# A fused attention and FFN kernel: the first batch's k norms by a transposing sum, its first weight load in narrower pieces, its folds in other banks

## The chip, the cores and the metric

The kernel runs on one core of one Trainium2 chip. The metric is the device time of one execution in microseconds (us); the figure to go by is the median of several runs. Engines: PE is TensorE's matmul, PEld its weight loads, DVE is VectorE, ACT is ScalarE, POOL is GpSimd, SP is SyncE. Both POOL and SP issue DMA transfers here.

## What is computed

Four batches of cross-covariance attention, and then a feed-forward network with a product of two projections:

```python
def _attn_ref(q, k, v, tau):          # q, k, v: (4, 5824, 256)
    qn = q / (np.linalg.norm(q, axis=1, keepdims=True) + 1e-06)
    kn = k / (np.linalg.norm(k, axis=1, keepdims=True) + 1e-06)
    s = kn.transpose(0, 2, 1) @ qn / tau
    s = s - s.max(-1, keepdims=True)
    a = np.exp(s)
    a /= a.sum(-1, keepdims=True) + 1e-09
    return (v @ a).astype(np.float32)

def _moe_ref(x, w1, w2, w3, w_out):   # w1, w2: (256, 1024); w3: (1024, 1024); w_out: (1024, 256)
    a = x @ w1
    b = x @ w2
    h = a * b @ w3
    return (h @ w_out).astype(np.float32)
```

The norms run over the 5824 tokens, so each batch has 256 norms of q and 256 of k, and its attention matrix is only 256x256. tau is 1.

## The kernel before

Three products are folded ahead of time. The attention matrix e (exponentials, not yet divided by their sums) goes into the first weights: Wf = e w1 and e w2, with the division in the eviction from PSUM. And w3 w_out is one matrix, W_sb. What is left for a batch is a loop over chunks of 512 tokens and over eight blocks of 128 hidden columns: two products a and b of v's transposed tokens with Wf (`emit_ab`, L656), their elementwise product on DVE (abh, L673, after ACT has copied a, L662), and the product of abh with W_sb. One pass over one block is called a slot. While a batch's loop runs, the next batch's scores and norms are put between its slots.

**The first batch** has no loop to hide in. Its q and k come in six pieces by DMAs that POOL issues, with a cast from fp32 to bf16; TensorE forms the products G = q^T k (`products`, L271) and the squares of q (`squares`, L259, the 128x128 products of each half with itself, of which the diagonal is wanted) as they arrive. The squares of k take two ways. For pieces 0 to 3 and half of piece 4, ACT squares and DVE adds into `kacc` (`add_k_squares`); the rest goes to TensorE into S["k"] like q's.

Then follow the steps of `soft_units(0)`, taken in the order written out by hand at L853 to L873: soft0[7] is `k_early` (the two halves of kacc added to the row kk), soft0[0] `k_first` (the diagonal of S["k"] times the identity, plus kk), soft0[1] `k_row`, soft0[2] `q_first` (the diagonal of S["q"], dq), soft0[3] `scaled_first` (G times kr, the norms of q, both halves of the exponentials e), soft0[6] `sum_start`, and soft0[4] `first_folds`. `k_row` multiplies by a matrix of ones, so that each partition has all 256 sums of squares, and takes the reciprocal norms by Ln and Exp in four steps of ACT over 128x256, kr. The remaining steps of the first batch are set among the first slots of the loop by `make_agenda` (L907 and following): soft0[5], `second_quarter`, ahead of the second slot, and the four folds of columns 512 to 1023 after it.

`first_folds` makes the folds of columns 0 to 127 and 128 to 255 (`narrow_fold`), `second_quarter` those of 256 to 511, and `fold(i)` for i = 4 to 7 those of the last 512 columns: i = 4 and 5 for w1, 6 and 7 for w2. All of the narrow folds of columns 0 to 255 stand in TensorE's queue ahead of the first slot of the loop.

**Later batches** have their norms another way: `norms` (L301) is a VectorE sum that transposes 32x32 blocks and sums along them, `totals` multiplies the 16 columns with `fold4` (four stacked identities of 32), four ACT steps work on 16 columns, and `spread` (L322) transposes the norms of k back into a row.

**Loads.** POOL issues all loads in one queue, and each waits, by one of eight semaphores in turn, until the load eight before it has landed. w1 and w2 come in three pairs (L844 to L846): columns 0 to 255, 256 to 511 and 512 to 1023. Ahead of them is the first half of v's first piece, behind them the second half, v's pieces 1 and 2, w_out and w3. SP issues DMA transposes (w3, and v from piece 2 on) and the stores. In the loop, `at(t, ...)` sets a step at a time t of a clock that counts TensorE's planned work; `gate` and `hold` let POOL wait for the loop or for a transpose before it issues a load.

**PSUM banks** come from `bank(tag)`: four in turn for "ab" (a and b of the slots, and other short-lived tiles), three in turn for "out". A tile waits until its bank's last tile has been evicted. In the first batch, `fold(i)` has the default tag "ab".

Of the kernel before, what the change touches and what calls it, by code (L numbers as in the profile page):

```python
# [9 lines left out]
AF = mybir.ActivationFunctionType  # L10
ALU = mybir.AluOpType
F32 = DT.float32
BF16 = DT.bfloat16

P = 128
# [10 lines left out]
def kernel(  # L26
# [12 lines left out]
    nc = tc.nc  # L39

    B, N, C = q.shape
    T, D = out.shape
    F = moe_w1.shape[1]
# [24 lines left out]
    work = ctx.enter_context(tc.tile_pool(name="work", bufs=2))  # L68
# [6 lines left out]
    def bank(tag):  # L75

        turns[tag] += 1
        return {"tag": f"{tag}{turns[tag] % (4 if tag == 'ab' else 3)}", "bufs": 1}
# [7 lines left out]
    ones_pp = consts.tile([P, P], F32)  # L86
# [3 lines left out]
    eps_t = consts.tile([P, 1], F32)  # L90
# [6 lines left out]
    fold4 = consts.tile([P, 4, 32], F32)  # L97
# [21 lines left out]
    def load_part(nm, n, pi, lo, hi):  # L119
        nc.gpsimd.dma_start(  # L120
            out=pieces[nm, n, pi][:, lo:hi, :], in_=qk_main[nm, n][0][:, pi * PIECE + lo : pi * PIECE + hi, :]
        )
# [10 lines left out]
    def new_vT(n):  # L133
        vTs[n] = (
            vT_pool.tile([P, NT - 1, CT, P], BF16, tag="vT", name=f"vT_{n}"),
            vT_pool.tile([P, CT, P + LEFT], BF16, tag="vTt", name=f"vTt_{n}"),
        )
# [22 lines left out]
    def transpose_piece(n, pi):  # L160
        if pi == 0:
            new_vT(n)
        vT, vTt = vTs[n]
        t = pieces.pop(("v", n, pi))
        if pi < NP_ - 1:
            nc.sync.dma_start_transpose(vT[:, pi * PIECE : (pi + 1) * PIECE, :, :], t[:, :, :])
        else:
            g = LAST - 1
            nc.sync.dma_start_transpose(vT[:, pi * PIECE : pi * PIECE + g, :, :], t[:, :g, :])

            first = n % 2 == 0
            nc.sync.dma_start_transpose(vTt[:, :, :P] if first else vTt[:, :, LEFT:], t[:, g, :])
            nc.sync.dma_start_transpose(vTt[:, :, P:] if first else vTt[:, :, :LEFT], t[:LEFT, g + 1, :])
# [3 lines left out]
    accs = {}  # L177
# [57 lines left out]
    kacc = []  # L235
# [41 lines left out]
    def soft_units(n):  # L277
        st = {}

        def k_early():  # L280
            st["kk"] = work.tile([P, C], F32, tag="kk", name="kk", bufs=1)
            nc.vector.tensor_copy(st["kk"], kacc[0][:, 0, :])
            nc.vector.tensor_add(st["kk"], kacc[0][:, 1, :], st["kk"])

        def k_first():
            d = work.tile([P, CT, P], F32, tag="sq", name="dk", bufs=2)
            nc.vector.tensor_mul(d, S["k"], ident.unsqueeze(1).to_broadcast([P, CT, P]))
            d = st["ksq"] = d.rearrange("p c t -> p (c t)")
            nc.vector.tensor_add(d, d, st["kk"])

        def scaled_first():
            for ct in range(CT):
# [2 lines left out]
            exps(0)  # L295
            exps(1)

        def norms():

            red = work.tile([P, 16], F32, tag="red", name=f"red_{n}", bufs=1)  # L300
            nc.vector.tensor_reduce(  # L301
                out=red, in_=accs[n].rearrange("p w (b j) -> p (w b) j", j=32),
                axis=mybir.AxisListType.X, op=ALU.add, apply_transpose=True,
            )
            st["red"] = red

        def totals():
# [3 lines left out]
            )  # L311

        def norm_step(i):
            t = st["tot"][:, :16]
            nc.scalar.activation(
                out=t, in_=t, func=(AF.Ln, AF.Exp)[i % 2],
                scale=(1.0, 0.5, 1.0, -1.0)[i], bias=eps_t if i == 2 else 0.0,
            )

        def spread():  # L320
            st["kr"] = work.tile([P, C], F32, tag="kr", name=f"kr_{n}", bufs=1)
            nc.vector.transpose(  # L322
                st["kr"].rearrange("p (b j) -> p b j", j=32),
                st["tot"][:, 8:16].unsqueeze(2).to_broadcast([P, 8, 32]),
            )

        def pick():
# [9 lines left out]
        def k_row():  # L337

            m = psum.tile([P, 512], F32, name=f"row_{n}", **bank("ab"))
            nc.tensor.matmul(m[:, :C], lhsT=ones_pp, rhs=st["ksq"], start=True, stop=True)  # L340
            st["row"] = m[:, :C]
            st["kr"] = work.tile([P, C], F32, tag="kr", name=f"kr_{n}", bufs=1)
            for i in range(4):
                k_step(i)

        def k_step(i):
            kr = st["kr"]
            nc.scalar.activation(
                out=kr, in_=kr if i else st["row"], func=(AF.Ln, AF.Exp)[i % 2],
                scale=(1.0, 0.5, 1.0, -1.0)[i], bias=eps_t if i == 2 else 0.0,  # L350
            )

        def diagonal(src):
            d = work.tile([P, CT, P], F32, tag="sq", name=f"dq_{n}", bufs=2)
# [26 lines left out]
        def exps(ct):  # L381
            if ct == 0:
                st["e"] = work.tile([P, CT, C], BF16, tag="e", name=f"e_{n}", bufs=2)
            nc.scalar.activation(
                out=st["e"][:, ct, :], in_=st["s"][:, ct, :], func=AF.Exp, scale=st["r"][:, ct : ct + 1]
            )
# [51 lines left out]
        def fold(i, tag="ab"):  # L438
            h, rest = divmod(i, 4)
            w, c1 = divmod(rest, 2)  # L440
            for c2 in range(CT):
                fold_mm((w, c1, h * 512, (h + 1) * 512), c2, tag, i % 2 == 0 or (n == 0 and i == 7))
# [31 lines left out]
                    narrow_fold(256, 512, c1, c2)  # L474

        if n == 0:
            return [k_first, k_row, q_first, scaled_first, first_folds, second_quarter, sum_start, k_early] + [lambda i=i: fold(i) for i in range(4, 8)]

        return (
            [(0.0, 0.0, norms), (0.1, 2.4, totals)]  # L480
# [21 lines left out]
    def at(t, cost, fn):  # L502
        seq[0] += 1
        agenda.append((t, seq[0], cost, fn))
# [336 lines left out]
    load_piece("q", 0, 5, (1, 3, 4))  # L841
    new_piece("v", 0, 0)
    load_part("v", 0, 0, 0, half)
    for f0, f1 in ((0, 256), (256, 512), (512, F)):  # L844
        nc.gpsimd.dma_start(out=w12[:, :, 0, f0:f1], in_=w1r[:, :, f0:f1])
        nc.gpsimd.dma_start(out=w12[:, :, 1, f0:f1], in_=w2r[:, :, f0:f1])  # L846
    load_part("v", 0, 0, half, PIECE)
# [59 lines left out]
    def make_agenda(b):  # L907
        agenda.clear()
        clock[0] = 0.0
        n = b + 1  # L910
        if b == 0:
            at(0.5, 0.87, soft0[5])
            for i in range(4):
                at((1.7, 2.6, 3.5, 3.9)[i], 0.43, soft0[8 + i])
            at(4.6, 0.5, lambda: transpose_half_on_pe(0, 0, 1, False))
            at(7.0, 0.5, lambda: transpose_half_on_pe(0, 1, 0, False))
            at(8.0, 0.5, lambda: transpose_half_on_pe(0, 1, 1, False))
            at(15.0, 0.0, transpose_w3)
            at(15.0, 0.0, lambda: transpose_piece(0, 2))
            for jt in range(FT):  # L920
                at(28.3 + 1.2 * jt, 0.87, lambda jt=jt: w_unit(jt))
            moves = [("qk", 1, 0, 29.0), ("qk", 1, 1, 29.2), ("v", 0, 3, 33), ("qk", 1, 2, 49), ("qk", 1, 3, 56)]
            moves += [("qk", 1, 4, 62), ("v", 0, 4, 68), ("qk", 1, 5, 79), ("v", 0, 5, 88)]
            moves += [("v", 1, 0, 99), ("v", 1, 1, 110), ("qk", 2, 0, 122)]
        else:
            moves = [("qk", n, 1, 1), ("v", b, 2, 7), ("qk", n, 2, 19), ("v", b, 3, 25), ("qk", n, 3, 37)]
            moves += [("v", b, 4, 43.5), ("qk", n, 4, 55.5), ("v", b, 5, 61), ("qk", n, 5, 72.5)]
            moves += [("v", n, 0, 85), ("v", n, 1, 98), ("qk", n + 1, 0, 111)]
            moves = [m for m in moves if m[1] < B]

        for nm, m, pi, t in moves:
            if nm == "qk" and m == 1 and pi in (0, 2):
                at(t, 0.0, lambda pi=pi: hold(vTs[0][0][:1, (2 + pi // 2) * PIECE, 0, :1]))
            at(t, 0.0, gate)
            if nm == "qk":
                at(t, 0.0, lambda m=m, pi=pi: load_qk(m, pi))
            else:
                at(t, 0.0, lambda m=m, pi=pi: load_piece("v", m, pi))
                at(t + 4.0, 0.0, lambda m=m, pi=pi: transpose_piece(m, pi))
        if b == 0:  # L940
            for i in range(4):
                at(COMB + 2.6 * i, 0.0, lambda i=i: combine_weights(i))
        if n == B:
            agenda.sort()
            return
        units = score_units(n)
        soft = soft_units(n)
        first, last = SLOTS if b > 0 else SLOTS0
        for s in range(first, last):
            lo_, hi_ = (share(b, x, first, last, len(units)) for x in (s, s + 1))  # L950
            by_slot.append((s, units[lo_:hi_]))

        def chain():
            for cst, t, fn in soft:
                at(clock[0] + 1.0 + t, cst, fn)
            agenda.sort()

        by_slot.append((last, [(0.0, chain)]))
        agenda.sort()
# [23 lines left out]
    n = len(pend)  # L983
# [37 lines left out]
```

## Time and profile before

| | us |
|---|---|
| median of 3 runs | 556.74 (555.41 to 557.5) |
| the profiled execution | 555.64 |
| its span, first to last instruction | 553.9 |
| first product of the loop (L656) starts | 37.12 |
| PE busy in the span | 542.9 (98%) |
| DVE, ACT, POOL busy | 435.3, 377.0, 305.5 |

The share of busy time is over the whole span. The page's row of DMA engines by fortieths shows how different the start is:

```profile
PE   8799999999999999999999999999999999999997
DMA  9999889986666878676554777865650245443102
```

Each digit is a slice of 13.8 us, in tenths. In the first four slices the DMA engines are at nine tenths or more; later they have room. A landing is the moment when a transfer's last packet is in; "issue" in the chain of waits is time in which nothing that the profile shows was waited for.

### The profile page before, as it was taken

The numbers are of one execution on the slowest core, as the hardware profiler recorded it, in microseconds if no ns is written. First come the engines' busy times: TensorE is split into PE (matmuls) and PEld (weight loads), VectorE is DVE, ScalarE is ACT, GpSimd is POOL, SyncE is SP. The second block draws the span as 40 slices with busy tenths as digits, with TensorE's granted clock in tenths as the row PEclk, the third lists the DMA queues.
The fourth block names the chain that finished last, engine by engine and source line by source line (L and its number), as shares of the span: only waits on it lengthen the run. The fifth ranks groups of instructions, "written<-read, shape, count | busy, mean of one in ns | idle before, by whom it ended". The sixth has DMA issues, their size and how long they took to land.

```text
span 553.9 us, 12324 instructions
## 1 busy us (share of the span) xinstructions
PE 542.9 (98%) x4623; PEld 353.3 (64%) x4630; DVE 435.3 (79%) x787; ACT 377.0 (68%) x757; POOL 305.5 (55%) x259
## 2 busy tenths in 40 slices
PE   8799999999999999999999999999999999999997
PEld 4564577766666666666667666666666666666665
DVE  5558747899976787988876788888877688888984
ACT  5446647788866777777766777777766666566663
POOL 4260021877889678889887588898987400010000
PEclk9999999999999999999999999999999999999999
DMA  9999889986666878676554777865650245443102
GB/s 214 211 178 209 168 160 207 214 206 90 160 130 155 191 150 162 126 148 138 127 128 121 153 152 158 167 141 120 151 115 40 83 114 119 92 111 80 77 40 96
DMA packets 75260, 77.61 MB, mean 140 GB/s; under 512 B 54208, under 2 KB 59072, under 8 KB 75200
## 3 DMA queue, kind: packets, MB, share of 16 engines
q0 software_dynamic: 15904, 38.93, 40.0%
q1 hardware_dynamic: 58928, 37.17, 24.5%
q8 instruction: 36, 0.59, 0.4%
q10 hardware_dynamic: 368, 0.72, 0.4%
q14 instruction: 24, 0.20, 0.1%
HBM read 78.91 MB, written 23.86 MB: 186 GB/s over the span
## 4 chain that ended last, share of the span: by engine, by line
PE 92%; DMA 6%; POOL 1%; DVE 0%; ACT 0%; issue 0%; POOLq 0%
PE a L656 28%; PE b L656 28%; PE prodA L569 12%; PE prodC L569 6%; PE G L200 5%; PE prodB L569 3%; DMA k<-in_k_dram 3%; PE o L704 3%; PE fold L427 2%; DMA q<-in_q_dram 2%; PE o_out L735 2%; PE w L878 1%; DMA w<-in_moe_w_dram 1%; PE narrow L451 0%; DVE abh L673 0%
## 5 line engine op out<-in xcount | busy, mean ns | idle before, releaser
L673 DVE TENSOR_TENSOR abh<-as,b 128x512 bf16<-128x512 bf16 x352 | 240.2, 684 | 82.9 <-ACT as L662 77.8
L662 ACT CAST as<-a 128x512 bf16<-128x512 f32 (+1 forms) x384 | 215.4, 562 | 93.7 <-PE a L656 61.5
L656 PE MATMUL a<-vT,Wf 128*128 128x512 bf16 x704 | 209.6, 380 | 0.1
L656 PE MATMUL b<-vT,Wf 128*128 128x512 bf16 x704 | 209.7, 380 | 0.0
L656 PEld LDWEIGHTS <-Wf 128*128 128x128 bf16 x1536 | 141.0, 98 | 100.7 <-issue 0.5
L569 PEld LDWEIGHTS <-S 128*128 128x128 bf16 x1248 | 82.6, 98 | 34.3
L212 DVE TENSOR_TENSOR acc<-acc,sq 128x512 f32<-128x512 f32 x132 | 91.6, 694 | 3.0 <-ACT sq L197 1.9
L579 ACT COPY osb<-prodA 128x256 f32<-128x256 f32 x156 | 58.1, 372 | 42.0 <-PE prodA L569 41.4
L588 POOL TENSOR_TENSOR S<-abh,abh 128x1024 bf16<-128x1024 bf16 x29 | 61.7, 2127 | 31.5 <-DVE abh L673 16.6
L569 PEld LDWEIGHTS <-abh 128*128 128x128 bf16 x936 | 61.9, 98 | 25.7 <-issue 0.2
L591 POOL TENSOR_TENSOR S<-S,abh 128x1024 bf16<-128x1024 bf16 x29 | 61.7, 2126 | 1.9
L591 POOL TENSOR_TENSOR S<-abh,S 128x1024 bf16<-128x1024 bf16 x29 | 61.8, 2133 | 0.1
L591 POOL TENSOR_TENSOR S<-abh 128x1024 bf16<-128x1024 bf16 x29 | 61.8, 2131 | 0.1
L644 POOL COPY gate_t<-abh 1x1 bf16<-1x1 bf16 x39 | 7.2, 185 | 79.9 <-DVE abh L673 79.7
L569 PE MATMUL prodA<-comb_T,S 128*128 128x128 bf16 x624 | 47.6, 220 | 0.0
L200 PE MATMUL G<-k,q 128*128 128x256 bf16 x276 | 47.0, 273 | 0.0
L197 ACT ACTIVATE sq<-q 128x512 f32<-128x512 bf16 x69 | 43.8, 634 | 0.0
L197 ACT ACTIVATE sq<-k 128x512 f32<-128x512 bf16 x69 | 43.4, 628 | 0.0
L582 DVE TENSOR_TENSOR osb<-prodC,osb 128x256 f32<-128x256 f32 x78 | 32.5, 417 | 0.0
L648 POOL COPY gate_t<-vT 1x1 bf16<-1x1 bf16 x2 | 0.4, 176 | 53.3 <-DMA vT<-v 53.3
L200 PEld LDWEIGHTS <-q 128*128 128x128 bf16 x276 | 23.9, 98 | 3.6
L569 PE MATMUL prodB<-W_sb,abh 128*128 128x128 bf16 x312 | 23.8, 220 | 0.1
(137 smaller groups left out, 469.8 us busy)
## 6 DMA issues: line engine op xcount, KB each, us to landing
out_dram<-osb SPq DMA_DIRECT2D x44, 512.0 KB, 3.3
k<-in_k_dram POOLq DMA_DIRECT2D x19, 512.0 KB, 8.7
v<-in_v_dram POOLq DMA_DIRECT2D x19, 512.0 KB, 5.6
q<-in_q_dram POOLq DMA_DIRECT2D x18, 512.0 KB, 5.4
w_wout<-in_moe_w_dram POOLq DMA_DIRECT2D x1, 2048.0 KB, 22.4
k<-in_k_dram POOLq DMA_DIRECT2D x4, 320.0 KB, 7.0
v<-in_v_dram POOLq DMA_DIRECT2D x4, 320.0 KB, 5.2
q<-in_q_dram POOLq DMA_DIRECT2D x3, 320.0 KB, 5.0
```

Source lines behind the costliest of these rows:

```text
L197: nc.scalar.activation(out=sqs[0][:, :, part, :], in_=src[:, o : o + 2, :], func=AF.Square)
L200: nc.tensor.matmul(G[:, ct, :], lhsT=qt[:, i, ct * P : (ct + 1) * P], rhs=kt[:, i, :], start=(pr == 0 and part == 0 and ct == 0), stop=(pr ...
L212: nc.vector.tensor_add(accs[n], accs[n], sqs[0][:, part - 2])
L569: nc.tensor.matmul(st[nm][:, i, :], lhsT=a[:, j, i * P : (i + 1) * P], rhs=w[j], start=(first and j == 0 and i == 0), stop=(j == 3), skip_ ...
L579: nc.scalar.copy(quarter(r, d), st["A"])
L582: nc.vector.tensor_add(quarter(r, d), st[nm], quarter(r, d))
L588: adder.tensor_add(x, a21, a22)
L591: adder.tensor_sub(x, u, w)
L656: nc.tensor.matmul(t[:, :n], lhsT=Wf[b][:, ct, w, j * P : (j + 1) * P], rhs=rhs_of(b, c, ct), start=(ct == 0), stop=(ct == CT - 1),)
L662: nc.scalar.copy(a_sb[:, :n], tiles[0][:, :n])
L673: nc.vector.tensor_mul(ab, a_sb, tiles[1])
L704: nc.tensor.matmul(t[:, k, :], lhsT=ab2[j // 4][:, j % 4, (2 * h + k) * P : (2 * h + k + 1) * P], rhs=W_sb[:, j, :], start=(j == 0 and k = ...
```

## The change

For the first batch:

1. The sums of squares of k are made with transposing sums on VectorE. `k_early` sums kacc to 16 columns and adds the two halves to 8; `k_first` sums the diagonal of S["k"] to 8 and adds. `k_row` multiplies these 8 columns with `fold4`, runs the four ACT steps on 8 columns in PSUM, and then spreads them to a row of 256 on VectorE.
2. The first pair of loads of w1 and w2 (256 columns) is two pairs of 128 columns: eight weight loads in place of six.
3. Folds 4, 5 and 6 take a bank of "out", fold 7 one of "ab".
4. The DMA transpose of v's piece 4 is set at 2.5 after its load on the planning clock, not 4.0.

```diff
         def k_early():
-            st["kk"] = work.tile([P, C], F32, tag="kk", name="kk", bufs=1)
-            nc.vector.tensor_copy(st["kk"], kacc[0][:, 0, :])
-            nc.vector.tensor_add(st["kk"], kacc[0][:, 1, :], st["kk"])
+            red = work.tile([P, 16], F32, tag="red", name="red_acc", bufs=1)
+            partition_sums(red, kacc[0].rearrange("p w (b j) -> p (w b) j", j=32))
+            st["kk"] = work.tile([P, 8], F32, tag="kk", name="kk", bufs=1)
+            nc.vector.tensor_add(st["kk"], red[:, :8], red[:, 8:])
 
         def k_first():
             d = work.tile([P, CT, P], F32, tag="sq", name="dk", bufs=2)
             nc.vector.tensor_mul(d, S["k"], ident.unsqueeze(1).to_broadcast([P, CT, P]))
-            d = st["ksq"] = d.rearrange("p c t -> p (c t)")
-            nc.vector.tensor_add(d, d, st["kk"])
+            red = work.tile([P, 16], F32, tag="red", name="red_end", bufs=1)
+            partition_sums(red[:, :8], d.rearrange("p c (b j) -> p (c b) j", j=32))
+            st["ksq"] = work.tile([P, 8], F32, tag="ksum", name="ksum", bufs=1)
+            nc.vector.tensor_add(st["ksq"], red[:, :8], st["kk"])
...
+        def partition_sums(dst, src):
+
+            nc.vector.tensor_reduce(out=dst, in_=src, axis=mybir.AxisListType.X, op=ALU.add, apply_transpose=True)
+
+        def root_step(t, i):
+
+            nc.scalar.activation(
+                out=t, in_=t, func=(AF.Ln, AF.Exp)[i % 2],
+                scale=(1.0, 0.5, 1.0, -1.0)[i], bias=eps_t if i == 2 else 0.0,
+            )
+
...
+        def spread(src=None):
+            src = st["tot"][:, 8:16] if src is None else src
             st["kr"] = work.tile([P, C], F32, tag="kr", name=f"kr_{n}", bufs=1)
             nc.vector.transpose(
                 st["kr"].rearrange("p (b j) -> p b j", j=32),
-                st["tot"][:, 8:16].unsqueeze(2).to_broadcast([P, 8, 32]),
+                src.unsqueeze(2).to_broadcast([P, 8, 32]),
             )
...
             m = psum.tile([P, 512], F32, name=f"row_{n}", **bank("ab"))
-            nc.tensor.matmul(m[:, :C], lhsT=ones_pp, rhs=st["ksq"], start=True, stop=True)
-            st["row"] = m[:, :C]
-            st["kr"] = work.tile([P, C], F32, tag="kr", name=f"kr_{n}", bufs=1)
+            t = m[:, :8]
+            nc.tensor.matmul(t, lhsT=fold4.rearrange("p g j -> p (g j)"), rhs=st["ksq"], start=True, stop=True)
             for i in range(4):
-                k_step(i)
+                root_step(t, i)
+            spread(t)
...
-            return [k_first, k_row, q_first, scaled_first, first_folds, second_quarter, sum_start, k_early] + [lambda i=i: fold(i) for i in range(4, 8)]
+            return [k_first, k_row, q_first, scaled_first, first_folds, second_quarter, sum_start, k_early] + [lambda i=i: fold(i, "ab" if i == 7 else "out") for i in range(4, 8)]
...
-    for f0, f1 in ((0, 256), (256, 512), (512, F)):
+    for f0, f1 in ((0, P), (P, 256), (256, 512), (512, F)):
         nc.gpsimd.dma_start(out=w12[:, :, 0, f0:f1], in_=w1r[:, :, f0:f1])
         nc.gpsimd.dma_start(out=w12[:, :, 1, f0:f1], in_=w2r[:, :, f0:f1])
...
-                at(t + 4.0, 0.0, lambda m=m, pi=pi: transpose_piece(m, pi))
+                at(t + (2.5 if (m, pi) == (0, 4) else 4.0), 0.0, lambda m=m, pi=pi: transpose_piece(m, pi))
```

The later batches call the same helpers with the same instructions as before.

## The prediction

> **What bounds the kernel now.** I read the page first, then busy time by stretches, then the chain of waits over the first 48 us, then the timeline there and the landing of each transfer.
>
> The stretches say where a change of the start can act at all:
>
> ```profile
> 0.00:37.12 37.12, 30.59 (x255) 21.09 (x257) 19.69 (x49) 16.69 (x30) 17.77 (x35) 1.00 1.05 201
> 37.12:46.48 9.36, 9.26 (x64) 5.25 (x65) 6.59 (x11) 6.35 (x11) 0.83 (x1) 1.00 1.12 202
> 46.48:84.00 37.52, 37.52 (x226) 21.75 (x224) 25.65 (x40) 21.02 (x38) 3.24 (x9) 1.00 0.95 177
> 84.00:553.90 469.90, 465.49 (x4084) 305.18 (x4087) 383.32 (x690) 332.98 (x680) 283.64 (x215) 1.00 0.59 131
> ```
>
> After the stretch's bounds and length come PE, PEld, DVE, ACT and POOL, the clock, the share of the 16 DMA engines and GB/s. From 37.12, the first product of the main loop, TensorE is full to the end. So the time is the start of the loop, plus a fixed 516 us of TensorE work, plus holes in it. The edits lie before 46.48, the loads among them in the last 17 us, where the DMA engines are over-full (1.05, 1.12). They can only move the loop's start or open and close holes behind it. The chain of waits there:
>
> ```profile
> 29.97 0.69 POOL w L845
> 30.67 5.22 DMA w<-in_moe_w_dram
> 35.89 0.04 issue
> 35.93 0.33 PE narrow L451 x3
> 36.26 0.03 PE sum L404 x2
> 36.29 0.26 PE narrow L451 x4
> 36.55 0.04 issue
> 36.59 0.48 ACT Wf L458
> 37.08 0.05 issue
> 37.12 0.61 PE a L656 x2
> ...
> 42.27 0.67 DVE Wf L436
> 42.94 0.04 issue
> 42.98 0.59 PE fold L427 x2
> ```
>
> The first fold waits for the second weight load (w2, columns 0 to 255), landing at 35.89. The timeline shows a tie: both halves of e are 34.98 + 0.91 = 35.89 as well. The last three lines are a hole: fold 7 waits for fold 5's eviction, since both use one bank. TensorE would have been free at 42.34 + 0.43 = 42.77, so 0.2 us is lost. What runs ahead:
>
> ```profile
> 31.07 0.60 PE L340 MATMUL row<-dk,ones_pp 128*128 128x256 f32 x2
> 33.11 0.42 ACT L348 ACTIVATE kr<-kr 128x256 f32<-128x256 f32 x1
> 33.46 0.29 DVE L357 CUSTOM_DVE_ANT_0 dq<-sqq,ident 128x128 f32<-128x128 f32 x1 [2.63 <-PE sqq L259]
> 33.89 0.75 DVE L379 TENSOR_TENSOR s<-G,kr 128x256 f32<-128x256 f32 x2
> 34.98 0.91 ACT L384 ACTIVATE e<-s,r 128x256 bf16<-128x256 f32 x2 [0.54 <-DVE r L371]
> ```
>
> kr is ready at 33.53, yet the scaling by kr starts at 33.89, behind dq, which waited for TensorE's squares of q (done 33.43). So the norms of k are not the last to arrive; the path is TensorE, dq, s, e. The row product sits in TensorE's queue ahead of those squares, and that is how it counts.
>
> Landings, as issue plus time to landing when each transfer is asked for alone: w1 and w2 of columns 0 to 255 at 29.97 + 4.2 = 34.2 and 35.89; of 256 to 511 at 31.38 + 4.9 = 36.3 and 32.07 + 6.0 = 38.1; of 512 to 1023 at 32.77 + 6.7 = 39.4 and 33.46 + 7.3 = 40.8; then v's pieces at 42.0, 44.4 and 46.9, w_out 49.6, w3 59.5. Needed: 35.9, 38.1 (second product of the quarter, 37.99 + 0.11), 39.75 (fold 4), about 41.5 (fold 6), 43.4 and 44.7 (v's transposes). So the whole stream is just in time, with 0 to 1.4 us of slack.
>
> **What the Trainium skill says.** "DMA: Bandwidth & Descriptors", Specifications, gives 512 B as the smallest transfer at line rate, with a read-modify-write below it. Its section "Why small descriptors are slow (HBM only)" makes the penalty a fixed cost per packet, 27% at 256 B. Here, before holds no 256 B load with a cast; its 256 B packets are DMA transposes, 1636 of them in 61 to 63 us, one per 20 ns and engine. So the two statements bound the cost, and the trace doesn't choose. "VectorE: DVE Perf Modes", the section on the errata of SBUF sources, gives (N+151)/0.96 ns for a fp32 operation on two tensors: 424 ns at N = 256, and the trace's 128x256 additions take 424.
>
> **The change part by part.**
>
> *Norms of k.* DVE loses a copy and two additions of 0.42. It gains a transposing sum of 128x512 (0.71, from the same operation in later batches, L301), one of 128x256 (not in the trace; between 0.42 by the rule above and 0.71; I take 0.45), two small additions (0.17, as tot at L330) and a spread (0.44, L322). The first sum and its addition run from 28.33 to about 29.25, in the gap before sqk (29.91): free. After dk's product, started at 29.95, the next operation can start at 30.41; 0.45 + 0.03 + 0.17 give 31.07, and TensorE reaches the row at 31.07: just hidden, at 0.71 TensorE is held 0.26. On TensorE the row takes 31.07 to 31.50 = 0.43; the 16-column product of later batches takes 0.20 of the queue. So TensorE gains 0.2 (between 0.25 and -0.05). ACT's four steps go from 1.8 us to four of 0.18 to 0.26 with gaps, about 1.0: from 31.47 to 32.45, spread to 32.9, before dq at 33.25. The spread stands ahead of dq on DVE but is done first. The pieces of q land from 30.9 to 32.2, each ahead of its new slot. So dq, s and e come 0.2 earlier: e at 35.7.
>
> *Loads.* Two pairs of 256 columns cover 512 now; after, two pairs of 128 come first, then 256 to 511, then the rest. From 33.0 to 35.5 the engines take 735 packets of 512 B: 54 ns each per engine. From 50 to 54, 415 packets of 2048 B: 154 ns. A line through both gives 21 ns + 0.065 per byte, so 38 ns at 256 B, an estimate. A load of 256 packets takes 16 of them per engine: 0.87 us at 512 B, 0.61 at 256 B. The first pair is 2 x 0.26 = 0.5 us earlier: 35.4, no longer last. The second narrow pair, which TensorE needs before the first loop product because the folds of columns 128 to 255 stand ahead of it, lands at 35.89 + 4 x 0.61 - 2 x 0.87 = 35.89 + 0.7 = 36.6. All later landings move by the same 0.7. Bounds: 0 if a packet costs its bytes alone, 1.7 if it costs what a 512 B packet does.
>
> Then: seven narrow products after 36.6, at 0.055, give the first loop product at 37.05 (before 37.12). It ends at 37.93, and the quarter fold needs w2 of 256 to 511, now 38.1 + 0.7 = 38.8, where it had waited for nothing. Seven products of 0.11 follow: the second loop product at 39.6, before 38.89: **0.7 later**. Note that this wait swallows the 0.2 of the norms. Further: fold 4 would run at 40.5 (w1 at 40.1), fold 6 at about 42.2 (w2 at 41.5): covered.
>
> *Queue of POOL.* Eight weight issues in place of six, 0.72 each, so v's other pieces, w_out and w3 are issued 1.4 us later. It is hidden as long as the engines have a backlog: v's second piece is issued at 34.69 and lands 9.7 us later, so 1.4 us is far less than its queueing.
>
> *Banks.* Folds 4 to 6 go to the "out" banks and fold 7 alone to an "ab" bank; fold 7 no longer waits for fold 5: **-0.2**. The "out" banks they take were evicted at 35.7, 39.3 and 39.8 before, plus 0.7, all ahead of their folds.
>
> *v's transposes.* In the order of the built program the SP queue of the two kernels is the same: piece 4's transpose stays between the same two stores with the same waits. **0**.
>
> Sum: +0.7 - 0.2 = **+0.5 us**. At 45.2 TensorE then transposes v's second piece, which lands at 45.1; piece 2's DMA transpose (68.92 + 5.2 = 74.1, behind w3's four) comes at 74.8, and TensorE wants it at 75.04 + 0.5. Both hold, narrowly. The profiled execution took 555.64 (span 553.9), so 556.1 on its basis; the median of the runs is 556.74, 1.1 above it, and on that basis, which I give, **557.2**.
>
> **Rivals.**
>
> *Bytes alone count.* Then nothing lands later; the second loop product is where it was (w2 of the quarter still 38.1), and -0.2 of the bank stays: 556.5. For it: the fast 256 B transposes. Against: the 21 ns that the line leaves at zero bytes.
>
> *The issue binds.* If the 1.4 us on POOL passes through, v's second piece lands at 44.4 + 1.4 = 45.8, where TensorE is ready at 45.2: 0.6 more, 557.8. Against: the DMA share over 1 throughout.
>
> *Slower.* Packets under 512 B pay for a read-modify-write and cost twice a 512 B one, 109 ns: the stream is late by 4 x 1.74 - 2 x 0.87 = 5.2 us, every need above follows it, and with -0.2 for the bank the time is about 561.7. It decides from 74 ns a packet (4 x 1.19 - 1.74 = 3.0). For it the skill's line; against it the transposes' 20 ns.
>
> *The norms do nothing.* If the sum of 128x256 takes 0.71, the row is late and the 0.2 is gone. The time stays 557.2, as the quarter's load is last anyway.
>
> **How the numbers follow.** About 0.5%, 2.8 us, is what a measurement of this kernel can tell from no change. My forecast, with the bounds of the packet's cost above it (up to +1.5) and the idle norms in it, gets 0.52; bytes alone 0.20; the issue 0.15; slower 0.10; 0.03 is left for a gain that I don't see. The first three are within 0.5%: 0.87. The range runs from bytes alone (556.5) less 0.9 for the spread of runs (555.4 to 557.5) to a packet at the 512 B price (558.2) plus 0.9: 555.6 to 559.1.
>
> **What would show it.** Right: w2 of columns 128 to 255 landing near 36.6 and of 256 to 511 near 38.8; a hole of 0.8 us on TensorE in the quarter fold; none before fold 7; the row at 0.2; e at 35.7; SP's order as before. Wrong: no hole there (bytes), a hole at v's second piece (issue), or the first loop product after 39 (read-modify-write).

## The result, and the profile after

| | before | after |
|---|---|---|
| median of the runs, us | 556.77 (555.41 to 558.0) | 558.2 |
| ratio of the two, with its interval | | 1.0024 (1.0016 to 1.0033) |
| the profiled execution, us | 555.64 | 558.31 |
| its span, us | 553.9 | 556.5 |
| first product of the loop starts, us | 37.12 | 36.73 |
| PE busy in the span, us | 542.9 | 542.9 |

The change costs 1.3 us by the ratio (0.0024 x 556.77), within the 0.5% that counts as no change here, though the ratio's interval leaves 1 out. Two of after's 20 runs, 572.5 and 952.82 us at a granted clock of 0.95 and 0.56, are not in the ratio. The two profiled executions differ by 2.67 us, about twice the medians' difference: the one of before lies near the low end of its own runs, that of after at its median. So the profile shows where time goes, and its amounts are those of one execution.

The stretches of after, cut at its own first product of the loop, with the columns as in the prediction (length, then PE, PEld, DVE, ACT and POOL busy, clock, share of the DMA engines, GB/s):

```profile
0.00:36.73 36.73, 30.27 (x255) 20.77 (x257) 20.45 (x51) 15.69 (x30) 17.79 (x35) 1.00 1.05 200
36.73:46.48 9.75, 7.59 (x43) 3.89 (x44) 5.15 (x8) 5.52 (x10) 2.21 (x3) 1.00 1.06 173
46.48:84.00 37.52, 36.87 (x227) 21.29 (x227) 25.38 (x39) 20.29 (x37) 3.53 (x9) 1.00 0.91 165
84.00:556.50 472.50, 468.14 (x4101) 306.99 (x4104) 385.02 (x693) 334.58 (x682) 283.69 (x215) 1.00 0.59 132
```

The loop starts 0.4 us earlier, and then PE is idle for 2.2 us of the second stretch (9.75 - 7.59), where it had been idle for 0.1. In the third stretch it misses another 0.65, where it had missed nothing. All the loss is behind the start of the loop and ahead of 84 us.

The norms first. In the timeline (start, length, engine, line, operation, output and input, and in brackets what it waited for), the steps from the sums of k to the exponentials:

```profile
28.26 0.72 DVE L303 TRANSPOSE_TENSOR_REDUCE red_acc<-kacc 128x16 f32<-128x512 f32 x1
30.34 0.45 DVE L303 TRANSPOSE_TENSOR_REDUCE red_end<-dk 128x8 f32<-128x256 f32 x1
31.04 0.39 PE L349 MATMUL row<-ksum,fold 128*128 128x8 f32 x2
...
32.32 0.45 DVE L330 STREAM_TRANSPOSE kr<-row 128x256 f32<-128x256 f32 x1 [1.34 <-ACT row L307]
33.25 0.29 DVE L358 CUSTOM_DVE_ANT_0 dq<-sqq,ident 128x128 f32<-128x128 f32 x1 [0.47 <-PE sqq L259]
...
34.74 0.91 ACT L385 ACTIVATE e<-s,r 128x256 bf16<-128x256 f32 x2 [0.51 <-DVE r L372]
```

The 128x256 sum takes 0.45, the row starts at 31.04 with the squares of q 0.25 behind it (0.43 before), dq starts at 33.25 (33.46), and e is complete at 34.74 + 0.91 = 35.65 (35.89).

Then TensorE behind it, in the same view:

```profile
36.73 0.60 PE L657 MATMUL a<-vT,Wf 128*128 128x512 bf16 x2
...
37.61 1.04 PE L452 MATMUL narrow<-w,e 128*128 128x256 bf16 x8
...
38.48 0.59 PE L657 MATMUL a<-vT,Wf 128*128 128x512 bf16 x2
...
41.62 0.59 PE L428 MATMUL fold<-w,e 128*128 128x512 bf16 x2 [2.11 <-DMA w<-in_moe_w_dram]
...
44.63 0.59 PE L428 MATMUL fold<-w,e 128*128 128x512 bf16 x2
...
77.68 0.60 PE L657 MATMUL a<-vT,Wf 128*128 128x512 bf16 x2 [0.54 <-DMA vT<-v]
```

The quarter fold (37.61) runs without a hole, and the second product a starts at 38.48, 0.41 earlier than before. The hole is at fold 4 (41.62): the first load of columns 512 to 1023 lands at 41.57, where it had landed at 39.43. TensorE's queue loses 2.27 us there. Before, fold 4 ran at 39.75, without a wait:

```profile
39.75 0.60 PE L427 MATMUL fold<-w,e 128*128 128x512 bf16 x2
```

Fold 7 (44.63) has no hole any more; before, it waited 0.2. Two small holes follow, 0.28 at v's second piece (it lands at 46.61) and 0.70 at 77.68, at the DMA transpose of v's piece 2. That transpose is issued behind w3's own, which wait for w3 to land: at 71.30; before, at 68.92. But the later issue alone doesn't make this last hole. The chain of waits of after shows the transpose with its length:

```profile
71.30 6.34 DMA vT<-v
```

It took 6.34 us, and 5.20 before. With 5.20 it would have been in at 76.50, ahead of TensorE, whose queue was free at 76.98. In the trace, 15 of the transpose's 16 completions are in by 76.08 and the last one at 77.64. Ahead of the transpose's last two packets of 4 B stands a packet of 16 KB of the queue that the profile calls "instruction", from 75.62 to 76.55. Five other profiles show the same order and a last completion as late, with the weights late or not (below). In the other eight no such packet comes ahead, and all 16 completions are in within 0.5 us. So the packet is very likely what holds the transpose up; no run moves it to show it, and what decides the order is open.

The account closes: -0.4 (start) + 2.27 + 0.28 + 0.70 - 0.2 (fold 7) = 2.65, and the copies of a on ACT are late by 2.65 from slot 32 to the end.

The chain of waits of after, from 28 us on, goes straight through POOL's queue:

```profile
29.91 0.70 POOL w L846
30.61 0.71 POOL w L847
31.33 0.71 POOL w L846
32.03 0.71 POOL w L847
32.74 0.70 POOL w L846
33.44 0.71 POOL w L847
34.15 0.70 POOL w L846
34.85 0.71 POOL w L847
35.56 0.47 POOL v L120
36.02 10.59 DMA v<-in_v_dram
46.61 0.05 issue
46.66 0.62 PE tr_I-609_610 L143 x8
```

Before, the chain named one issue of w2 and its transfer. Here it is eight weight issues in a row, 0.7 us each, whether 128, 256 or 512 columns wide. The two added ones put the wide loads and v's pieces 1.33 us later on POOL. The issue of w1's columns 512 to 1023, in POOL's timeline of before and then of after:

```profile
32.77 0.73 POOL L845 DMA_DIRECT2D w<-in_moe_w_dram  x1
```

```profile
34.10 0.75 POOL L846 DMA_DIRECT2D w<-in_moe_w_dram  x1
```

The landings in after: the eight weight loads at 33.80, 34.16, 35.33, 35.54, 37.00, 37.58, 41.57 and 42.86, v's pieces at 44.17, 46.61 and 49.02, w_out at 51.68, w3 at 61.63. So columns 256 to 511 of w2 are in 0.5 us earlier than before, and all that follows is 2.1 to 2.2 us later.

### The profile page after: what moved, and what is told of

It is laid out like the page before. It is cut to its first block, busy times and chain, and to the rows that moved or that the text cites. A ratio compares the mean times of both kernels' runs of the same rounds, so it can differ in the third digit from the quotient of the medians.

```text
span 556.5 us, 12329 instructions
## 1 busy us (share of the span) xinstructions
PE 542.9 (98%) x4623; PEld 352.9 (63%) x4630; DVE 436.0 (78%) x789; ACT 376.1 (68%) x757; POOL 307.2 (55%) x261
## 4 chain that ended last, share of the span: by engine, by line
PE 89%; DMA 8%; POOL 2%; issue 0%; DVE 0%; ACT 0%; SPq 0%; POOLq 0%
PE a L657 28%; PE b L657 28%; PE prodA L570 12%; PE prodC L570 6%; PE G L200 5%; PE prodB L570 3%; DMA k<-in_k_dram 3%; PE o L705 3%; DMA v<-in_v_dram 2%; PE fold L428 2%; DMA q<-in_q_dram 2%; PE o_out L736 2%; DMA vT<-v 1%; POOL w L847 1%; POOL w L846 1%; PE w L879 0%
```

## The experiments

What had to be told apart: is it the loads or another edit; if the loads, is it their number, POOL's time for issuing them, the narrow packets, or what POOL does meanwhile. The expectations use letters for theories: A, the loads alone make the loss; B, the other edits disturb the loads; I, two further issues pass through to everything behind them; C, POOL's work for w_out and w3 disturbs the transfers that run at the time; S, the engines get too little to do while POOL issues narrow loads; T, or P, the narrow packets themselves are the cost. All runs were repeated in five rounds beside before.

This table is put together from the traces: the load of w1's columns 512 to 1023, the first wide one, and what the kernels took.

| run | that load issued, us | landed, us | between | w3 lands, us | ratio to before |
|---|---|---|---|---|---|
| before | 32.77 | 39.43 | 6.66 | 59.46 | |
| after | 34.10 | 41.57 | 7.47 | 61.63 | 1.0024 (1.0016 to 1.0033) |
| after, repeated | 34.34 | 41.16 | 6.82 | 61.61 | 1.0018 (1.0005 to 1.0031) |
| loads only | 34.37 | 41.47 | 7.10 | 61.66 | 1.0016 (1.0006 to 1.0026) |
| after, with a hold | 34.22 | 40.22 | 6.00 | 60.72 | 1.0016 (1.0007 to 1.0025) |
| before, POOL pause | 34.20 | 40.81 | 6.61 | 60.73 | 1.0009 (0.9998 to 1.0019) |
| after without the loads | 32.94 | 39.51 | 6.57 | 59.45 | 0.9996 (0.9986 to 1.0006) |
| before, with a hold | 33.12 | 40.23 | 7.11 | 60.25 | 1.0001 (0.9988 to 1.0013) |
| six loads, one narrow pair | 33.17 | 39.80 | 6.63 | 60.52 | 1.0003 (0.9990 to 1.0016) |

Issue times differ by a few tenths between executions of the same order, since POOL's queue starts its last stretch at 29.2 to 29.7.

### The loads alone, and all but the loads

Before with only the new loads:

```diff
-    for f0, f1 in ((0, 256), (256, 512), (512, F)):
+    for f0, f1 in ((0, P), (P, 256), (256, 512), (512, F)):
```

> The kernel before with the narrower weight loads alone (eight loads, the first two pairs of 128 columns). In the changed kernel's trace the first six weight loads came early and the seventh, w1 of columns 512 to 1023, landed at 41.57 us and not 39.43, with all later loads 2.1 us late. Theory A (the loads alone do it): here too that load lands about 41.5, w3 about 61.5, fold 4 waits over 1.5 us, and the time is 558.2 to 558.6, the change's own loss plus the 0.2 to 0.4 that the other edits gave back. Theory B (the norms and banks shift VectorE's or TensorE's work so that the loads are disturbed): the loads land as before, w3 at 59.5, and the time is 556.8.

Measured: 557.88 against 556.81, ratio 1.0016 (1.0006 to 1.0026). In its timeline, the same hole at fold 4:

```profile
41.52 0.61 PE L427 MATMUL fold<-w,e 128*128 128x512 bf16 x2 [1.40 <-DMA w<-in_moe_w_dram]
```

It loses 1.56 us there, 0.21 at fold 7 as before does, and 0.85 at the transpose of v's piece 2, which again takes long (6.52 us). The landings are those that A gives; the time is 0.3 under A's range.

After with the loads of before:

```diff
-    for f0, f1 in ((0, P), (P, 256), (256, 512), (512, F)):
+    for f0, f1 in ((0, 256), (256, 512), (512, F)):
```

> The changed kernel with the weight loads of before (six loads). Theory A: w1 of columns 512 to 1023 at about 39.4, w3 about 59.5, no wait at fold 4 or fold 7, and the time is 0.2 to 0.4 under before, 556.4. The first loop product does not come earlier than about 36.9, since w2 of columns 0 to 255 lands at 35.9. Theory B: the loads are late as in the changed kernel, w3 about 61.5, time about 558.

Measured: 556.63 against 556.81, ratio 0.9996 (0.9986 to 1.0006). No hole at any fold, the first product of the loop at 36.97, and the landings are those of before. So the loads make the loss, all of it within what can be measured, and the other three edits together make no difference that can be measured.

After itself was run once more, beside the last experiments.

> The changed kernel once more, on the chip of the other three, for its landings in a second execution: w1 of columns 512 to 1023 at 41.0 to 42.0, fold 4 waiting 1.5 to 2.5 us, time 557.9 to 558.5. If the load lands before 40.5, the late landing of the first profile was an accident of that execution.

Measured: 557.98 against 556.42, ratio 1.0018 (1.0005 to 1.0031), with the hole at fold 4 again:

```profile
41.20 0.59 PE L428 MATMUL fold<-w,e 128*128 128x512 bf16 x2 [1.27 <-DMA w<-in_moe_w_dram]
```

The holes here are 1.44 at fold 4 (a little under what was expected), 0.24 at v's second piece and 1.24 at piece 2's transpose (6.52 us long). The places are the same; their sizes change from one execution to the next. The earlier start of the loop is not repeated: the first narrow load of w2 lands at 35.92 here, not 34.16, and the loop starts at 37.15.

### Eight issues, none narrow

Before, with eight loads of 256 columns each:

```diff
-    for f0, f1 in ((0, 256), (256, 512), (512, F)):
-        nc.gpsimd.dma_start(out=w12[:, :, 0, f0:f1], in_=w1r[:, :, f0:f1])
-        nc.gpsimd.dma_start(out=w12[:, :, 1, f0:f1], in_=w2r[:, :, f0:f1])
+    for w, f0 in ((0, 0), (1, 0), (0, 256), (1, 256), (0, 512), (0, 768), (1, 512), (1, 768)):
+        nc.gpsimd.dma_start(out=w12[:, :, w, f0 : f0 + 256], in_=(w1r, w2r)[w][:, :, f0 : f0 + 256])
```

> The kernel before with eight weight loads of 256 columns each, so that no packet is under 512 B: w1 and w2 of 0 to 255, then of 256 to 511, then w1 of 512 to 767 and 768 to 1023, then w2 of these. Theory P (narrow packets are the price): v's pieces, w_out and w3 land within 0.4 us of before (w3 59.2 to 59.9) and the time is 556.5 to 557.0. Theory I (the two more issues of 0.7 us on POOL's queue are the price): v's second piece and w3 land 1.4 to 2.2 us later than before (w3 60.9 to 61.7), and the time is 557.8 to 558.6.

Measured: 556.32 against 556.81, ratio 0.9993 (0.9982 to 1.0003). POOL issues eight times as in after, the last weight load at 35.14, and yet all weights are in by 40.07 (40.78 before) and v's second half at 42.07 (42.01 before). Two more issues by themselves cost nothing, so theory I, as it was put, falls; the landings are those that P gives. What the same eight issues carry decides: after six of them three quarters of the weights are issued here, and half in after. The stretch from 36.5 to 39, with the columns as above, of before:

```profile
36.50:39.00 2.50, 2.36 (x22) 1.59 (x20) 1.52 (x3) 1.77 (x4) 1.45 (x2) 1.00 1.08 164
```

the same stretch of after:

```profile
36.50:39.00 2.50, 2.36 (x17) 1.48 (x16) 1.62 (x4) 1.81 (x4) 2.44 (x4) 1.00 0.92 95
```

and of this kernel with eight equal loads:

```profile
36.50:39.00 2.50, 2.36 (x25) 1.65 (x25) 1.37 (x4) 1.48 (x4) 2.34 (x4) 1.00 1.39 179
```

The last two numbers of each line are the ones to read. With times of issue that differ by under 0.4 us, the engines move 179 GB/s with eight equal loads and 95 with the narrow ones first (105 in the repeated run). A share over 1 means that packets overlap in an engine; at 0.92 there is on average less than one in each. A share of 0.92 looks like a full engine, and isn't one.

Eight equal loads were also put into after, twice, and once with a hold on w_out:

> The changed kernel with eight weight loads of 256 columns (w1 and w2 of 0 to 255 and 256 to 511, then both of w1, then both of w2): the candidate that may beat both. Under theories S and T alike: all weights by 40.1, w3 by 59.7, no wait at folds 4 and 7, and 0.4 to 0.7 us under before: 556.1 to 556.4.

> The changed kernel with eight weight loads of 256 columns once more, to narrow its interval: all theories 556.0 to 556.4, a ratio of 0.9985 to 0.9995 to before, w3 by 59.8.

> The same with POOL waiting for the last weight load before w_out and w3. Theory C: the packets of 34 to 38 us, some of which took 0.5 to 1 us in the run without the wait, are steadier and all weights land by 39.8, time 555.8 to 556.2. Theory I: no change against the run without the wait.

Measured: 556.22, ratio 0.9990 (0.9980 to 1.0001); 556.8, ratio 0.9996 (0.9980 to 1.0011); and 556.41, ratio 0.9994 (0.9982 to 1.0006). In all three every weight is in by 39.8 to 40.6. No interval leaves 1 out: this is no proven gain over before, and the second run's 556.8 is above what was expected. The hold did not bring the weights in by 39.8, as C had it (40.63). In the second and third profile the transpose of v's piece 2 takes 6.37 and 6.31 us, and TensorE waits 0.64 and 0.79 for it, though every weight is in and w3 lands at 59.31 and 60.05. So that hole comes without late weights too.

### Supply or narrow packets

A pause in place of the two added issues, in before, with its own packet sizes: POOL copies 128x512 twice between the first and the second pair (idle_t is a tile that nothing else uses).

```diff
+        if f0 == 0:
+            for _ in range(2):
+                nc.gpsimd.tensor_copy(idle_t, warm)
```

> The kernel before with two copies of 128x512 on POOL (1.2 to 2 us, an estimate) between its first and second pair of weight loads, so that the same loads with the same packets come from POOL later, about as late as in the changed kernel. Theory S (supply: the engines move what POOL has issued faster than it issues, the backlog is gone, and the loads after it run slowly while POOL still makes descriptors): w1 of columns 512 to 1023 lands after 40.5 and w3 between 60.3 and 61.7, the time is 557.4 to 558.6. Theory T (packets under 512 B are what costs, through the engines' later work): the loads come at most 0.5 us later than before, w3 by 59.9, time 556.6 to 557.2.

POOL's timeline of this kernel shows the pause:

```profile
30.14 0.71 POOL L846 DMA_DIRECT2D w<-in_moe_w_dram  x1
30.84 0.72 POOL L847 DMA_DIRECT2D w<-in_moe_w_dram  x1
31.56 1.30 POOL L850 COPY idle_t<-warm 128x512 bf16<-128x512 bf16 x2
32.80 0.70 POOL L846 DMA_DIRECT2D w<-in_moe_w_dram  x1
33.49 0.71 POOL L847 DMA_DIRECT2D w<-in_moe_w_dram  x1
34.20 0.71 POOL L846 DMA_DIRECT2D w<-in_moe_w_dram  x1
```

and TensorE's timeline of it shows what follows at fold 4:

```profile
40.86 0.60 PE L428 MATMUL fold<-w,e 128*128 128x512 bf16 x2 [0.95 <-DMA w<-in_moe_w_dram]
```

Measured: 557.26 against 556.76, ratio 1.0009 (0.9998 to 1.0019). The wide load is issued 1.43 later than in before and lands 1.38 later, all that follows 1.3, w3 1.3. There is no narrow packet among its weight loads, and the hole at fold 4 is there (1.12 us of the queue), as is one at piece 2's transpose (0.67, the transpose takes 6.44). The landings are those of S. The time lies between the ranges of T and S, 0.1 from each, and its interval just touches 1. So the shift of the landings and the hole are what this run shows; that POOL's time makes the whole loss of after is not shown.

The counterpart: narrow packets, but late in the row. Of these eight loads, which replace the three pairs, the sixth and the eighth have 128 columns:

```diff
+    for w, f0, f1 in (
+        (0, 0, 256), (1, 0, 256), (0, 256, 512), (1, 256, 512), (0, 512, 896), (0, 896, F), (1, 512, 896), (1, 896, F)
+    ):
+        nc.gpsimd.dma_start(out=w12[:, :, w, f0:f1], in_=(w1r, w2r)[w][:, :, f0:f1])
```

> The kernel before with eight weight loads in which the narrow ones come last: columns 0 to 255 and 256 to 511 as before, then w1 of 512 to 895 and of 896 to 1023, then the same of w2. Two loads have 256 B packets, at a place where the backlog is deep. Theory S: no loss, w3 by 59.9, time 556.3 to 557.0. Theory T: half of the change's loss, w3 60.3 to 60.8, time 557.2 to 557.8.

Measured: 556.5 against 556.76, ratio 0.9997 (0.9986 to 1.0009). All weights are in by 41.06, v at 42.30, 44.81 and 47.25, w3 at 59.75. In this execution the first load of w2 was itself late (37.19) and made a hole of 1.23 ahead of the loop. Two narrow loads behind others that are still running cost nothing that can be measured, and w3 came when S has it: T falls at this place. With the pause above, this speaks for the place of the narrow loads and not their width.

One narrow pair with the number of issues unchanged:

```diff
-    for f0, f1 in ((0, 256), (256, 512), (512, F)):
+    for f0, f1 in ((0, P), (P, 512), (512, F)):
```

> The kernel before with six weight loads cut at 128 and 512: the first pair narrow, the second of 384 columns. POOL issues no more loads than before. Theory S: the wide second pair restores the backlog, w3 lands by 59.9; TensorE waits for w2 of 128 to 511 in the folds of 128 to 255 (first loop product about 37.6) and finds the next fold's weights there; time 556.7 to 557.4. Theory T: w3 60.3 to 60.8, fold 4 waits about 0.5 us more, time 557.3 to 558.2.

Measured: 556.9 against 556.76, ratio 1.0003 (0.9990 to 1.0016). Its wide load was issued 0.40 later than in before, because its queue started late, and landed 0.37 later. w3 came at 60.52, which is in T's range and not in S's. But w_out, just ahead of it, landed 0.28 later than in before, and the rest is w3's own load: 10.64 us behind w_out, and 9.86 in before. That distance is 9.84 to 10.78 over all the kernels here, so w3's landing doesn't decide for T. As the table shows, the 6.63 us from issue to landing are those of before. It has other holes, 0.47 and 0.90 at the narrow folds, since columns 128 to 511 of w2 come in one load at 38.03, and its loop started at 38.46, not at 37.6 as expected.

### What POOL does meanwhile

In after, POOL works on the issues of w_out and w3 from 37.07 to 38.95, in the middle of the slow stretch. Here POOL is held until the last weight is in:

```diff
     load_piece("v", 0, 2)
+    hold(w12[:1, CT - 1, 1, F - 1 :])
     nc.gpsimd.dma_start(out=wout_sb, in_=moe_w_out.rearrange("(lh ll) c -> ll lh c", ll=P))
```

> The changed kernel with POOL waiting for the last of the eight weight loads before it issues w_out and w3. Theory C (POOL's making of descriptors for w_out and w3, at 37.1 to 39.0 in the changed kernel, slows the engines' packets of the last weight pair, which take up to 2 us each there): w1 of columns 512 to 1023 lands at 40.0 or before, fold 4 waits under 0.7 us, time 556.4 to 557.0. Theory I (what is issued late lands late, whatever POOL does afterwards): that load lands at about 41.5 as in the changed kernel, fold 4 waits about 2 us, time 558 or more.

Measured: 557.65 against 556.81, ratio 1.0016 (1.0007 to 1.0025). The wide load lands 6.00 after its issue, the shortest of all, at 40.22, between what C and I expect, and two holes are left:

```profile
40.27 0.59 PE L428 MATMUL fold<-w,e 128*128 128x512 bf16 x2 [0.68 <-DMA w<-in_moe_w_dram]
...
45.83 0.62 PE L143 MATMUL tr_I-610_611<-ident_b,v 128*128 128x128 bf16 x8 [0.56 <-DMA v<-in_v_dram]
```

The time is not regained. In its stretch from 36.5 to 39 POOL is busy for 0.79, and the engines move 142 GB/s, where after and its repeated run have 95 and 105:

```profile
36.50:39.00 2.50, 2.36 (x19) 1.41 (x16) 1.62 (x4) 1.88 (x4) 0.79 (x2) 1.00 1.09 142
```

This could be read for C, so the same hold was put into before:

> The kernel before with POOL waiting for the last weight load before it issues w_out and w3. Theory C (POOL's making of descriptors slows packets in flight where the backlog is thin): before's own slow stretch from 35.5 to 38 us is shorter, w1 of columns 512 to 1023 lands at 39.0 or before (39.4 before), w2 at 40.3 or before (40.8), time 556.2 to 556.6. Theory I (supply alone): landings within 0.2 us of before, time 556.6 to 557.0.

Measured: 556.89 against 556.42, ratio 1.0001 (0.9988 to 1.0013). The stretch from 36.5 to 39 of this kernel:

```profile
36.50:39.00 2.50, 2.36 (x26) 1.67 (x25) 1.22 (x4) 1.42 (x3) 0.00 (x0) 1.00 1.02 144
```

POOL is idle (0.00), and the engines move 144 GB/s, less than before's 164 with POOL busy for 1.45. The wide load took 7.11 and landed 0.8 later than in before, which neither theory had expected. So a slow stretch comes with POOL idle too, and for before's loads C is not supported. For after's loads it stays open: the 6.00 with the hold lies outside what the other eight rows have in the column "between" (6.57 to 7.47), but it is one execution.

### What is shown, and what is open

Shown: the loads alone make the loss (first pair of runs); two more issues alone don't make it, nor do narrow packets at the two other places that were tried; a pause on POOL in their place moves the landings and opens the hole in the same way. How much of the time this explains is not shown: the pause cost 1.0009, the kernels with after's loads 1.0016 to 1.0024.

The reading that holds all nine rows of the table together: the first wide load lands 6.0 to 7.5 us after its issue, median 6.7, whatever POOL spent its time on ahead of it. It is therefore late by what POOL was late: in after 1.33 us, plus 0.81 for its own longer time; in the repeated run 1.57 plus 0.16; with the pause 1.43 less 0.05. Only where the last 512 columns come in smaller loads, as in the eight-wide kernels and in the one with the narrow loads last, is the later issue made good. In the eight-wide kernels those land 4.65 to 5.49 us after their issue, and all eight are in by 39.8 to 40.6, where before's six are in by 40.78. And from the wide load on the engines are the bound: in before and after, the next ones follow at 1.35 and 1.29, then 1.23 and 1.31, 2.42 and 2.44, 2.45 and 2.41. Its delay is handed on whole to v, w_out and w3.

Open: why the first wide load needs some 7 us when each later one needs 1.3. Its packets run slowly in a stretch with less than one packet in flight per engine: single 1024 B packets of after last up to 2.08 us there, where their median is 98 ns. No run takes this stretch apart. The 0.8 us that after has on top of the 1.33 is not settled either; runs of the same loads give from -0.66 (with the hold) to +0.81. And of the 2.65 us of after's profile, the 0.70 at piece 2's transpose go with its late last completion; the later landings alone would not have made them.

## Why the prediction was right, and where it was wrong

The sign, the class (within 0.5%) and the range held: 557.2 was forecast and 558.2 measured. The sum's +0.5 should have been +1.3. That it came out so near is partly luck: the +0.7 in it was set at the quarter fold, where none of the runs with these loads has a hole, and the loss came at fold 4, which the prediction had called covered.

**Norms of k.** Right in each term: 0.45 for the unknown sum, the row's 0.25 on TensorE (0.20 forecast), e at 35.65 (35.7), and nothing of it left at the end; the run without the loads shows no difference that can be measured.

**Loads.** The packet was sized near enough: 38 ns of an engine's time were forecast, and from 32.5 to 34.25 after's engines take 895 packets of 256 B, one per 31 ns and engine (a single one lasts 41). What failed is the sentence "All later landings move by the same 0.7". The step reckoned with engines that are the bound throughout. The last loads of columns 0 to 127 and 128 to 255 came at 34.16 and 35.54, not 35.4 and 36.6 (35.92 and 36.45 in the repeated run, near the forecast), and those of 256 to 511 of w2 at 37.58 and 38.08, not 38.8. So the hole of 0.8 in the quarter fold doesn't exist, and the loop began at 36.73 and 37.15, where 37.05 was forecast. The wide loads moved by 2.1, not 0.7.

**Queue of POOL.** This is the step that failed: "It is hidden as long as the engines have a backlog". The backlog was taken from shares of 1.05 and 1.12 over stretches of 37 and 9 us, and from the 9.7 us between the issue and the landing of v's second piece. In after that piece is issued 1.33 later and needs 10.59, so its wait swallowed nothing. Two narrow loads keep the engines busy for about 1.0 us (2 x 16 packets an engine at 31 ns) and cost POOL 1.4. Two loads of 256 columns take 1.74 by the prediction's own row, against 1.4; in the kernel with eight equal loads the time from issue to landing stays at 4.9 to 5.2 from the second load to the last, so they about keep pace with their issue. That the split removed a lead of the loads over the engines is argued from this, not shown. The prediction had both numbers and did not set them against each other. So the later issue passed through. In place of +0.7 - 0.2, the profiled execution has +2.65 and the medians +1.43.

**Banks.** Right: the hole of 0.2 at fold 7 is gone in after and is still there (0.21) in the kernel with the loads alone.

**v's transposes.** No run tests this part alone; its 0 is argued from the order of the SP queue, not shown.

**What holds "narrowly".** v's second piece costs 0.28: it came 2.18 later while TensorE came 1.65 later, and the slack was used up. Piece 2's transpose costs 0.70, though its later issue would still have held (76.50 against 76.98); the 0.70 come with the transpose's own 6.34 us, where the prediction had 5.2. The prediction named both places.

**The rivals.** "The issue binds" (557.8) has the mechanism, and its place is one load too late: the first to feel it is the wide load of w1, not v's second piece. "Bytes alone count" is refuted by the later landings, and by the 41 ns of a 256 B packet, which are not half of the 60 of a 512 B one. The read-modify-write that the Trainium skill's "DMA: Bandwidth & Descriptors", Specifications, states below 512 B was priced by the prediction at twice a 512 B packet; with 41 ns at 256 B and 60 at 512 B it is not seen here. These sizes are those written, in bf16; the fp32 columns read are twice as long.

## What to carry to other kernels

When one engine issues the loads one after another, set each load's time on the DMA engines against its time of issue: here the loads that took less than that (0.5 us against 0.7), first in the row, brought their own data forward and moved everything behind the next pair back. A DMA share near 1 over a long stretch does not prove a backlog; look at the GB/s in short stretches and at the time from issue to landing. Check the landing of every later load, since the loss here came three loads behind the ones that were split. And where a wait hangs on a transfer, check the transfer's own length before putting the wait down to its later issue.

## What the runs showed of the hardware

An issue on POOL costs 0.70 to 0.77 us for a weight load of 128, 256 or 512 columns; its time doesn't shrink with the width.

Packets of the casting loads last 41 ns at 256 B, 60 at 512, 98 at 1024, 173 at 2048 and 324 at 4096 (medians in after's trace): a fixed 22 ns and 0.074 ns per byte by the line through the first and the last. That is of the kind that the Trainium skill's "DMA: Bandwidth & Descriptors", section "Why small descriptors are slow (HBM only)", describes, a fixed cost per packet; the size differs, 27% there for a 256 B descriptor and 22 of 41 ns here.

The DMA transpose of v's piece 2 took 4.69 to 5.24 us in eight profiles and 6.31 to 6.52 in six; in those six a packet of 16 KB of the queue "instruction", 0.93 to 0.96 us long, stands in the trace ahead of its last packets.

A transposing sum of 128x256 takes 0.45 us, and one of 128x512 takes 0.72: half the columns is 0.63 of the time.
